# Block-local attention ahead of two expert layers: two query tiles at a time from tile 8 on

## The chip, the core and the metric

The kernel runs on one core of one Trainium2 chip. The metric is the device time of one execution in microseconds (us). TensorE (PE) multiplies matrices into PSUM, VectorE (DVE), ScalarE (ACT) and GpSimd (POOL) do the rest, and SyncE (SP) issues the transfers. Each engine runs its own instructions strictly in the order in which they were written, and waits at the head of its queue until another engine or a transfer has signalled.

## What is computed

Three stages follow one another. The attention is cut here to what matters; the other two only consume its output.

```python
# q, k, v: (2, 8, 768, 64); block 32, window 16
k_sum = k.reshape(B, H, nb, block, D).max(axis=3)
v_sum = v.reshape(B, H, nb, block, D).mean(axis=3)
scores_l = scale * q @ k^T, kept where abs(i - j) < window
scores_s = scale * q @ k_sum^T + log(block)
a = softmax(concat([scores_l, scores_s]))
attn = a @ concat([v, v_sum])
...
x  = attn as (1536, 512); x = sum over 8 experts of P[:, e] * (relu(x @ w1[e]) @ w2[e])
out = g(x @ w_in) @ w_out      # g a rational function
```

## The kernel before

**Tiles.** The 1536 rows of the attention are 24 query tiles of 64 rows, 12 in each batch entry (`QB = 12`). A tile `t` goes through five functions:

- `scores(t)`: 8 matmuls into a two-bank PSUM tile (`sc`), then 4 DVE reductions with the mask that write `a` and the row maxima `sm`.
- `exps(t)`: 4 ACT exponentials of `a`.
- `norm(t)`: three small DVE steps (add, reciprocal, multiply of `a`). Up to tile 16 their small results lie in spare columns of the bank of the last `xo` tile, later in `sm`.
- `trans(t)`: 4 PE transposes of `a` into a `tr` bank (`at`), and an ACT copy to `aT`. There are two `tr` banks, also used by half of the key and query transposes (`kps`, `qps`).
- `av(t)`: 8 matmuls of `aT` with the values `vx[t % 3]` into the only `xo` bank; an ACT cast to `xh` and a DVE difference to `xl`. `load_vx(t + 3)` then refills that value buffer by a transfer.

Each value is held as a rounded part and a remainder (`xh` and `xl`, `hh` and `hl`, `w2h` and `w2l`), and each product of the expert layers is three matmuls (lines 184 to 186).

**The main work.** The first expert's matmuls are cut into halves of 6 matmuls (`mains`): first-layer halves (`g1_halves`, 256 columns, written `p1`) and second-layer halves (`g2_halves`, 512 columns, `p2`). `share` says how many halves go with a step: 2, except 1 in steps 17, 18, 22 and 23. They fill PE between the attention's small matmuls. What empties a finished first-layer bank (ACT `hh`, DVE `hl`: a post) is put off: `flush()` writes it out at the next `av` or at the second half of the next product. The banks come from a pool of three (`psm`, `mm`), which the other half of the key and query transposes uses too.

**Order.** The program is written out by hand, step by step. Step `s` is: `scores(s)`, `av(s - 3)`, `flush()`, half the main work (before tile 12), `trans(s - 2)`, `norm(s - 1)`, `exps(s)`, then the step's list `todo[s]`, then the rest of the main work. `todo` holds the preparation of the second batch entry: key tiles are transposed and placed in steps 7 to 9 (`prep_k`), their edges copied and block maxima built in steps 8 to 10 (`halos`, `block_keys`, `blocks_to`), the means of its values in steps 9 to 13 (`sum_v`, `means_split`, `means_sum`, `block_values`), the second-layer weights split in steps 8 and 9 (`split_w2`), and query tiles placed in steps 10, 14 and 18 (`prep_q`).

Of the kernel before, what the change touches and what calls it, by code (L numbers as in the profile page):

```python
# [22 lines left out]
def kernel(  # L23
# [342 lines left out]
    with ExitStack() as actx:  # L366
# [229 lines left out]
        def load_vx(t):  # L596
# [5 lines left out]
                v[b, :, c0:c1, :].rearrange("h p d -> p h d"),  # L602
            )

        def scores(t):
            b, r = divmod(t, QB)
            qt = qT[b, r // TPL]
            if t == 1:
                ps = [psa.tile([P, NP, P], F32, tag="tr", name=f"sc_{t}_{x}", bufs=2) for x in range(2)]
            else:  # L610
                ps = psa.tile([P, 2, NP, P], F32, tag="sc", name=f"sc_{t}")
                ps = [ps[:, x] for x in range(2)]
            w = kw[:, slot(t)]
            i = 0 if r == 0 else (2 if r == QB - 1 else 1)
            m = masks[i]
            o = r % TPL * QT
            for p in range(NP):
                x = p % 2
                p = x * (NP // 2) + p // 2
                for j in range(2):  # L620
                    h = slice(j * D, (j + 1) * D)
                    y = (j ^ x) * D
                    nc.tensor.matmul(
                        ps[x][y:y + D, p % (NP // 2), 0:CO], lhsT=qt[h, p, o:o + QT], rhs=w[h, p, :],
                        start=True, stop=True, tile_position=(j * D, y),
                    )
            a = apool.tile([P, NP, CO], F32, tag="a", name=f"a_{t}", bufs=3)
            sm = apool.tile([P, 4, NP], F32, tag="sm", name=f"sm_{t}", bufs=3)
            for p in range(NP):
                p = p % 2 * (NP // 2) + p // 2  # L630
                nc.vector.tensor_tensor_reduce(
                    out=a[:, p, :], in0=ps[p // (NP // 2)][:, p % (NP // 2), 0:CO], in1=m[:, 0, :],
                    scale=-1.0, scalar=3.0e38, op0=ALU.add, op1=ALU.min, accum_out=sm[:, 0, p:p + 1],
                )
            st[t] = (a, sm, a)
# [32 lines left out]

        def av(t):
            aT = st.pop((t, "aT"))  # L670
            if t < 4 and t % 2:
                ps = psm.tile([P, NP * P], F32, tag="mm", name=f"xo_{t}").rearrange("p (c n) -> p c n", c=NP)
            else:
                ps = psa.tile([P, NP, P], F32, tag="xo", name=f"xo_{t}")
            for p in range(NP):
                for j in range(2):
# [4 lines left out]
                        rhs=aT[:, y:y + QT],  # L681
                        start=True, stop=True,
                    )
            st["xo"] = ps
            o = t * QT
            dh, dl = xh[:, :, o:o + QT], xl[:, :, o:o + QT]
            nc.scalar.copy(dh, ps[:, :, 0:QT])
# [142 lines left out]
            at(10 + i, means_split, i)  # L830
        at(13, means_sum)
        for t in range(QB, QB + 3):
            at(2 + t, block_values, t)
        at(13, gate_weights)
        at(13, gate_zeros)
        at(15, gate_parts)
# [7 lines left out]
        at(15, dma_sub, 0, 2)  # L844


        AV = 3
        mains = []
        for t0, n in ((0, 2 * P), (2 * P, 2 * P), (4 * P, 2 * P), (NT - HB, HB), (HT, HB)):
            ready = (t0 + n) // QT + AV  # L850
# [5 lines left out]
                    mains.append((ready, 0, f, NCH, h))  # L856
        share = dict(zip(range(7, 26), (2, 2, 2, 2, 2, 2, 2, 2, 2, 2, 1, 1, 2, 2, 2, 1, 1, 2, 2)))

        def main(s, end):
            n = share.get(s, 0)  # L860
            apart = n == 2 and s < QB
            for _ in range((1 if apart else n) if end else int(apart)):
                assert mains[0][0] <= s
                mains.pop(0)[2]()

        for s in range(NQ + AV):
            if s == 2:
                norm(0)
            if s < NQ:
                scores(s)  # L870
            if s == 2:
                prep_v(0, 0)
                prep_v(0, 1)
# [10 lines left out]
                prep_q(0, 1)  # L884
            if s >= AV:
                av(s - AV)
                if s - AV + 3 < NQ:
                    load_vx(s - AV + 3)
                flush()
            main(s, False)  # L890
            if AV < s < NQ + AV - 1:
                trans(s - AV + 1)
            if 2 < s < 6:
                spin(3)
            if AV < s <= NQ:
                norm(s - 1)
            if s < NQ and s not in (2, AV):
                exps(s)
            for f in todo.pop(s, []):
                f()  # L900
            main(s, True)
        assert not todo
        flush()
        assert not mains[0][4]
# [554 lines left out]
```

## Time and profile before

| | |
|---|---|
| time, median of 3 runs | 1352.11 us (1351.78 to 1352.18) |
| time of the profiled execution | 1352.21 us |
| its span, first to last instruction | 1350.5 us |
| busy share of the span: PE, DVE, ACT, POOL | 99%, 78%, 38%, 60% |
| share of the chain that ended last: PE, DVE, DMA | 97%, 1%, 1% |
| steps 8 to 23 of the attention | from 35.56 to about 95 us |

The profile lists, for one execution, what each engine did and when. Times of rows are us from the start of the span. The chain that ended last goes back from the last instruction to what released it, and so on: work off that chain can take longer at no cost. A matmul's record overlaps the next one's, so what a matmul costs is read from the distance of two starts, not from its duration; the same holds for neighbouring instructions of DVE and ACT.

### The profile page before, as it was taken

The page shows a single profiled execution, that of the slowest core. Times are in us where ns is not written, and L with a number is a line of the kernel's source. Part 1 is how long each engine was busy: PE and PEld are TensorE (multiplying, and loading weights), DVE is VectorE, ACT ScalarE, POOL GpSimd, SP SyncE. Part 2 cuts the span into 40 slices and gives each one's busy share as a digit, 9 for nine tenths or more (in the row PEclk, how much of TensorE's full clock was granted, in tenths as well). Part 3 has the DMA queues.
Part 4 walks back from the last instruction along what each step waited for, and adds up shares of the span by engine and source line. Part 5 has one row for each costly group of instructions (what it writes and reads, how often), then busy time and mean ns, then how long its engine had stood idle before and what let it go on. Part 6 is the DMA issues. An engine that isn't in the chain of part 4 may idle for free.

```text
span 1350.5 us, 20263 instructions
## 1 busy us (share of the span) xinstructions
PE 1342.1 (99%) x7343; PEld 1186.0 (88%) x7343; DVE 1052.9 (78%) x1956; ACT 510.9 (38%) x1136; POOL 804.3 (60%) x983
## 2 busy tenths in 40 slices
PE   8999999999999999999999999999999999999999
PEld 6888898999999999999999999999999888888887
DVE  7775588777777777777787777777777689988885
ACT  6874313222222222222222222222222379866662
POOL 7625747777776777776777767777777012222221
PEclk9999999999999999999999999999999999999999
DMA  9730112222222222222222222222222411312102
GB/s 262 169 85 1 51 46 63 89 70 79 67 73 68 67 77 67 83 66 87 69 77 72 67 74 68 76 69 77 75 80 62 146 57 47 94 33 94 32 16 78
DMA packets 122004, 102.40 MB, mean 76 GB/s; under 512 B 36272, under 2 KB 102960, under 8 KB 121904
## 3 DMA queue, kind: packets, MB, share of 16 engines
q1 hardware_dynamic: 121904, 101.10, 25.7%
q8 instruction: 58, 0.95, 0.3%
q14 instruction: 42, 0.34, 0.1%
HBM read 81.15 MB, written 19.92 MB: 75 GB/s over the span
## 4 chain that ended last, share of the span: by engine, by line
PE 97%; DVE 1%; DMA 1%; ACT 0%; SPq 0%; issue 0%; POOL 0%; DVEq 0%; ACTq 0%
PE p_v L185 12%; PE p_v L184 12%; PE p_v L186 12%; PE p L184 8%; PE p L186 8%; PE p L185 8%; PE X L1234 6%; PE X L1232 6%; PE X L1233 6%; PE Z L1233 3%; PE Z L1234 3%; PE Z L1232 3%; PE Y L1234 2%; PE Y L1233 2%; PE Y L1232 2%; PE xo L678 1%
## 5 line engine op out<-in xcount | busy, mean ns | idle before, releaser
L1347 DVE SCALAR_TENSOR_TENSOR accs<-p_v,Pt,accs 128x512 f32<-128x512 f32 x336 | 244.4, 746 | 85.9 <-PE p_v L186 85.2
L184 PE MATMUL p_v<-w2h_v,hh_v 128*128 128x512 f32 x720 | 282.2, 392 | 0.1
L186 PE MATMUL p_v<-w2h_v,hl_v 128*128 128x512 f32 x720 | 281.9, 392 | 0.0
L185 PE MATMUL p_v<-w2l_v,hh_v 128*128 128x512 f32 x720 | 281.7, 391 | 0.0
L1241 DVE SCALAR_TENSOR_TENSOR hl_v<-s,hh_v 128x384 fp32r<-128x384 f32 x180 | 137.4, 763 | 76.0 <-ACT hh_v L1240 74.6
L234 POOL TENSOR_TENSOR hl<-ta,hh 128x512 fp32r<-128x512 f32 x48 | 62.5, 1302 | 204.4 <-ACT hh L233 150.0
L1252 ACT COPY s<-X 128x384 f32<-128x384 f32 x56 | 27.0, 482 | 406.6 <-PE X L1234 406.6
L1041 POOL TENSOR_SCALAR ce<-ce 128x296 uint32<-128x296 uint32 (+1 forms) x56 | 67.1, 1199 | 176.7 <-DVE ce L1032 176.7
L186 PEld LDWEIGHTS p_v<-w2h_v,hl_v 128*128 128x128 f32 x720 | 135.2, 188 | 28.3
L184 PEld LDWEIGHTS p_v<-w2h_v,hh_v 128*128 128x128 f32 x720 | 135.4, 188 | 26.3 <-DVE accs L1342 0.5
L185 PEld LDWEIGHTS p_v<-w2l_v,hh_v 128*128 128x128 f32 x720 | 135.3, 188 | 25.9
L1240 ACT ACTIVATE hh_v<-s 128x384 fp32r<-128x384 f32 x180 | 94.9, 527 | 126.8 <-DVE s L1275 68.6
L110 POOL TENSOR_TENSOR wS<-S,wS 128x256 fp32r<-128x256 f32 x120 | 100.2, 835 | 14.4 <-ACT wS L107 4.7
L184 PE MATMUL p<-xh,w1h 128*128 128x512 f32 (+2 forms) x272 | 100.8, 371 | 0.0
L186 PE MATMUL p<-xh,w1l 128*128 128x512 f32 (+2 forms) x272 | 99.1, 364 | 0.0
L185 PE MATMUL p<-xl,w1h 128*128 128x512 f32 (+2 forms) x272 | 99.1, 364 | 0.0
L184 PE MATMUL p<-w2h,hh 128*128 128x512 f32 (+1 forms) x240 | 94.0, 392 | 0.0
L186 PE MATMUL p<-w2h,hl 128*128 128x512 f32 (+1 forms) x240 | 93.3, 389 | 0.0
L185 PE MATMUL p<-w2l,hh 128*128 128x512 f32 (+1 forms) x240 | 93.2, 388 | 0.0
L110 POOL TENSOR_TENSOR w2l_v<-sb,w2h_v 128x512 fp32r<-128x512 f32 x60 | 82.9, 1382 | 5.0
L1234 PE MATMUL X<-th,wS 128*128 128x384 f32 x240 | 80.3, 335 | 0.0
L1232 PE MATMUL X<-th,wS 128*128 128x384 f32 x240 | 80.3, 335 | 0.0
(249 smaller groups left out, 3309.1 us busy)
## 6 DMA issues: line engine op xcount, KB each, us to landing
sa<-in_moe_w_dram SPq DMA_DIRECT2D x30, 512.0 KB, 3.4
sb<-in_moe_w_dram SPq DMA_DIRECT2D x30, 512.0 KB, 4.3
cv<-in_moe_w_in_dram SPq DMA_DIRECT2D x24, 296.0 KB, 2.9
w1h<-f_in SPq DMA_DIRECT2D x16, 256.0 KB, 2.8
w1l<-f_in SPq DMA_DIRECT2D x16, 256.0 KB, 3.2
w2h<-f_out SPq DMA_DIRECT2D x16, 256.0 KB, 4.9
w2l<-f_out SPq DMA_DIRECT2D x16, 256.0 KB, 5.1
vx<-in_v_dram SPq DMA_DIRECT2D x20, 192.0 KB, 4.2
```

Source lines behind the costliest of these rows:

```text
L110: nc.gpsimd.tensor_sub(lo, src, hi.bitcast(F32))
L184: nc.tensor.matmul(ps, lhsT=sh, rhs=mh, start=(i == 0), stop=False)
L185: nc.tensor.matmul(ps, lhsT=sh, rhs=ml, start=False, stop=False)
L186: nc.tensor.matmul(ps, lhsT=sl, rhs=mh, start=False, stop=(i == n_k - 1))
L234: nc.gpsimd.tensor_sub(hl[:, :n], ta, hh[:, :n].bitcast(F32))
L1041: nc.gpsimd.tensor_scalar(out=e, in0=e, scalar1=896, scalar2=0, op0=ALU.subtract, op1=ALU.max)
L1232: nc.tensor.matmul(ps, lhsT=w[:, 0, t], rhs=mh, start=start and t == 0, stop=False, **go)
L1233: nc.tensor.matmul(ps, lhsT=w[:, 0, t], rhs=ml, start=False, stop=False, **go)
L1234: nc.tensor.matmul(ps, lhsT=w[:, 1, t], rhs=mh, start=False, stop=t == 1, **go)
L1240: nc.scalar.activation(hh, src, AF.Relu)
L1241: nc.vector.scalar_tensor_tensor(out=hl, in0=src, scalar=0.0, in1=hh.bitcast(F32), op0=ALU.max, op1=ALU.subtract)
L1347: nc.vector.scalar_tensor_tensor(out=a, in0=ps, scalar=Pt[:, g, e:e + 1], in1=a, op0=ALU.mult, op1=ALU.add)
```

## The change

From tile 8 on, steps are taken in pairs (`pair(s)` for even `s`). A pair is: `scores(s)`, `scores(s + 1)`, `exps(s)`, `av(s - 3)`, `av(s - 2)`, `norm(s)`, `flush()`, a quarter of the pair's main work, `exps(s + 1)`, `trans(s - 1)`, a quarter, `todo[s]`, a quarter, `trans(s)`, `todo[s + 1]`, a quarter, `norm(s + 1)`. The second tile's scores take the two `tr` banks in place of the two `sc` banks, and the odd tiles' `av` takes a bank of the pool of three. Before the first pair `trans(6)` and `norm(7)` are brought forward. The values of the block means (`block_values`) are copied a step earlier. No arithmetic is added or removed.

```diff
@@ -602,10 +602,13 @@
                 v[b, :, c0:c1, :].rearrange("h p d -> p h d"),
             )
 
+        AV = 3
+        PAIR = 8
+
         def scores(t):
             b, r = divmod(t, QB)
             qt = qT[b, r // TPL]
-            if t == 1:
+            if t == 1 or t > PAIR and t % 2:
                 ps = [psa.tile([P, NP, P], F32, tag="tr", name=f"sc_{t}_{x}", bufs=2) for x in range(2)]
             else:
                 ps = psa.tile([P, 2, NP, P], F32, tag="sc", name=f"sc_{t}")
@@ -668,7 +671,7 @@
 
         def av(t):
             aT = st.pop((t, "aT"))
-            if t < 4 and t % 2:
+            if t % 2 and (t < 4 or t >= PAIR - 3):
                 ps = psm.tile([P, NP * P], F32, tag="mm", name=f"xo_{t}").rearrange("p (c n) -> p c n", c=NP)
             else:
                 ps = psa.tile([P, NP, P], F32, tag="xo", name=f"xo_{t}")
@@ -681,7 +684,8 @@
                         rhs=aT[:, y:y + QT],
                         start=True, stop=True,
                     )
-            st["xo"] = ps
+            if t < PAIR - 3 or t % 2 == 0:
+                st["xo"] = ps
             o = t * QT
             dh, dl = xh[:, :, o:o + QT], xl[:, :, o:o + QT]
             nc.scalar.copy(dh, ps[:, :, 0:QT])
@@ -830,7 +834,7 @@
             at(10 + i, means_split, i)
         at(13, means_sum)
         for t in range(QB, QB + 3):
-            at(2 + t, block_values, t)
+            at(1 + t, block_values, t)
         at(13, gate_weights)
         at(13, gate_zeros)
         at(15, gate_parts)
@@ -844,7 +848,6 @@
         at(15, dma_sub, 0, 2)
 
 
-        AV = 3
         mains = []
         for t0, n in ((0, 2 * P), (2 * P, 2 * P), (4 * P, 2 * P), (NT - HB, HB), (HT, HB)):
             ready = (t0 + n) // QT + AV
@@ -856,18 +859,45 @@
                     mains.append((ready, 0, f, NCH, h))
         share = dict(zip(range(7, 26), (2, 2, 2, 2, 2, 2, 2, 2, 2, 2, 1, 1, 2, 2, 2, 1, 1, 2, 2)))
 
-        def main(s, end):
-            n = share.get(s, 0)
-            apart = n == 2 and s < QB
-            for _ in range((1 if apart else n) if end else int(apart)):
+        def main(s, n):
+            for _ in range(n):
                 assert mains[0][0] <= s
                 mains.pop(0)[2]()
 
-        for s in range(NQ + AV):
+        def pair(s):
+            n = [share[s], share[s + 1]]
+            two = s < NQ
+            if two:
+                scores(s)
+                scores(s + 1)
+                exps(s)
+            for t in (s, s + 1):
+                av(t - AV)
+                if t < NQ:
+                    load_vx(t)
+            if two:
+                norm(s)
+            flush()
+            main(s, n[0] // 2)
+            if two:
+                exps(s + 1)
+            trans(s - 1)
+            main(s, n[0] - n[0] // 2)
+            for f in todo.pop(s, []):
+                f()
+            main(s + 1, n[1] // 2)
+            if two:
+                trans(s)
+            for f in todo.pop(s + 1, []):
+                f()
+            main(s + 1, n[1] - n[1] // 2)
+            if two:
+                norm(s + 1)
+
+        for s in range(PAIR):
             if s == 2:
                 norm(0)
-            if s < NQ:
-                scores(s)
+            scores(s)
             if s == 2:
                 prep_v(0, 0)
                 prep_v(0, 1)
@@ -884,21 +914,27 @@
                 prep_q(0, 1)
             if s >= AV:
                 av(s - AV)
-                if s - AV + 3 < NQ:
-                    load_vx(s - AV + 3)
+                load_vx(s)
                 flush()
-            main(s, False)
-            if AV < s < NQ + AV - 1:
+            main(s, int(share.get(s) == 2))
+            if AV < s:
                 trans(s - AV + 1)
             if 2 < s < 6:
                 spin(3)
-            if AV < s <= NQ:
+            if AV < s:
                 norm(s - 1)
-            if s < NQ and s not in (2, AV):
+            if s not in (2, AV):
                 exps(s)
             for f in todo.pop(s, []):
                 f()
-            main(s, True)
+            main(s, int(share.get(s) == 2))
+        trans(PAIR - 2)
+        norm(PAIR - 1)
+        for s in range(PAIR, NQ + 2, 2):
+            pair(s)
+        av(NQ - 1)
+        for f in todo.pop(NQ + 2, []):
+            f()
         assert not todo
         flush()
         assert not mains[0][4]
```

Three places show how instructions move. The names end in the tile's number and a running number: `sc_9_1_703` is the second bank of tile 9's scores, `at_6` tile 6's transposes, `xo_5` its `av`, `p1_0_0_1` the first-layer product of the first rows with weight column 1, `a_8` tile 8's exponentials.

PE, where step 7 ends. Before:

```order
L186 MATMUL p1_0_0_0_0_626<-xh_90,w1l_0_0_480 128x256
L623 MATMUL sc_8_677<-kw_102,qs0_106 64x120 x8
L678 MATMUL xo_5_692<-aT_5_638,vx2_105 64x64 x8
L184 MATMUL p1_0_0_1_0_706<-xh_90,w1h_0_1_482 128x256
L185 MATMUL p1_0_0_1_0_706<-xl_91,w1h_0_1_482 128x256
L186 MATMUL p1_0_0_1_0_706<-xh_90,w1l_0_1_483 128x256
L184 MATMUL p1_0_0_1_0_706<-xh_90,w1h_0_1_482 128x256
L185 MATMUL p1_0_0_1_0_706<-xl_91,w1h_0_1_482 128x256
L186 MATMUL p1_0_0_1_0_706<-xh_90,w1l_0_1_483 128x256
L659 MATMUL at_6_713<-ident_84,a_6_547 120x128 x4
```

Now:

```order
L186 MATMUL p1_0_0_0_0_626<-xh_90,w1l_0_0_480 128x256
L662 MATMUL at_6_677<-ident_84,a_6_547 120x128 x4
L626 MATMUL sc_8_687<-kw_102,qs0_106 64x120 x8
L626 MATMUL sc_9_0_702<-kw_102,qs0_106 64x120 x2
L626 MATMUL sc_9_1_703<-kw_102,qs0_106 64x120 x2
L626 MATMUL sc_9_0_702<-kw_102,qs0_106 64x120 x2
L626 MATMUL sc_9_1_703<-kw_102,qs0_106 64x120 x2
L681 MATMUL xo_5_722<-aT_5_638,vx2_105 64x64 x8
L681 MATMUL xo_6_734<-aT_6_682,vx0_103 64x64 x8
```

Tile 6's transposes stand ahead of tile 8's scores, tile 9's scores follow at once in the two `tr` banks, and two `av` stand together.

ACT, from step 8 to the scores of tile 10 (`hh_0_0_1` is the post of `p1_0_0_1`, `w2h` the second-layer weights, `kw` the keys). Before:

```order
L687 CAST xh_90<-xo_6_777 128x4x64
L262 ACTIVATE hh_0_0_1_760<-p1_0_0_1_0_706 128x256
L661 COPY aT_7_803<-at_7_798 120x512
L641 ACTIVATE a_9_771,sm_9_772<-a_9_771,sm_9_772 128x120 x4
L440 ACTIVATE kw_102<-kps_1_2_0_818 128x16x32
L107 CAST w2h_0_2_830<-s2_0_1_651 128x512
L107 CAST w2h_0_3_834<-s2_0_1_651 128x512
L687 CAST xh_90<-xo_7_862 128x4x64
L262 ACTIVATE hh_0_0_2_845<-p1_0_0_2_0_791 128x256
```

Now, from tile 9's exponentials on:

```order
L644 ACTIVATE a_9_712,sm_9_713<-a_9_712,sm_9_713 128x120 x4
L664 COPY aT_7_767<-at_7_762 120x512
L440 ACTIVATE kw_102<-kps_1_1_0_784 128x16x32
L107 CAST w2h_0_0_796<-accs_92 128x512
L107 CAST w2h_0_1_800<-accs_92 128x512
L664 COPY aT_8_816<-at_8_811 120x512
L440 ACTIVATE kw_102<-kps_1_2_0_824 128x16x32
L107 CAST w2h_0_2_836<-s2_0_1_651 128x512
L107 CAST w2h_0_3_840<-s2_0_1_651 128x512
L262 ACTIVATE hh_0_0_1_775<-p1_0_0_1_0_751 128x256
L644 ACTIVATE a_10_867,sm_10_868<-a_10_867,sm_10_868 128x120 x4
L691 CAST xh_90<-xo_7_893 128x4x64
```

The post `hh_0_0_1` stood ahead of `aT_7` and of all that follows; now it stands behind two `aT`, two key copies and the four weight casts, and tile 10's exponentials behind it.

DVE, the same stretch (`hl_0_0_1` is the other half of that post, `ks` the block maxima, the three rows with `sm` and `a` a `norm`, ISA a reduction of scores). Before:

```order
L688 TENSOR_TENSOR xl_91<-xo_6_777,xh_90 128x4x64
L263 SCALAR_TENSOR_TENSOR hl_0_0_1_761<-p1_0_0_1_0_706,hh_0_0_1_760 128x256
L651 TENSOR_SCALAR xo_6_777<-sm_8_687 128x4
L652 RECIPROCAL xo_6_777<-xo_6_777 128x4
L653 TENSOR_TENSOR a_8_686<-a_8_686,xo_6_777 128x480
L480 TENSOR_REDUCE ks_1_655<-kw_102 128x4x8
L438 TENSOR_SCALAR kw_102<-kps_1_2_1_824 128x16x32
L631 ISA a_10_856,sm_10_857<-sc_10_847,mask1_111 128x120
```

Now:

```order
L480 TENSOR_REDUCE ks_1_655<-kw_102 128x4x8
L438 TENSOR_SCALAR kw_102<-kps_1_2_1_830 128x16x32
L263 SCALAR_TENSOR_TENSOR hl_0_0_1_776<-p1_0_0_1_0_751,hh_0_0_1_775 128x256
L654 TENSOR_SCALAR xo_6_734<-sm_9_713 128x4
L655 RECIPROCAL xo_6_734<-xo_6_734 128x4
L656 TENSOR_TENSOR a_9_712<-a_9_712,xo_6_734 128x480
L634 ISA a_10_867,sm_10_868<-sc_10_858,mask1_111 128x120
```

`hl_0_0_1` stood ahead of the block maxima and the key copy and now stands behind them; the `norm` of tile 9 and the reductions of tile 10 wait behind it.

## Rows read from the trace of the kernel before

**Rows 1.** Windows: steps 8 to the last `av`; us, then busy us of each engine.

```profile
35.56:102.79 67.23, 67.05 (x872) 56.48 (x871) 49.61 (x218) 53.63 (x201) 28.67 (x38) 1.00 0.52 120
102.79:1350.50 1247.71, 1244.40 (x6131) 1105.91 (x6127) 976.64 (x1625) 432.31 (x848) 749.94 (x881) 1.00 0.22 68
```

**Rows 2.** Timeline of PE, end of step 7: start, duration, line, tiles, count.

```profile
35.23 0.28 PE L185 MATMUL p<-xl,w1h 128*128 128x256 f32 x1
35.35 0.28 PE L186 MATMUL p<-xh,w1l 128*128 128x256 f32 x1
35.56 0.64 PE L623 MATMUL sc<-kw,qs 64*64 64x120 f32 x16
```

**Rows 3.** Timeline of PE, step 15, and a second-layer half of step 11.

```profile
65.71 0.64 PE L623 MATMUL sc<-kw,qs 64*64 64x120 f32 x16
66.28 0.69 PE L678 MATMUL xo<-aT,vx 120*64 120x64 f32 x16
66.90 0.65 PE L659 MATMUL at<-ident,a 128*120 128x128 f32 x4
67.31 0.36 PE L184 MATMUL p<-xh,w1h 128*128 128x256 f32 x1
67.51 0.28 PE L185 MATMUL p<-xl,w1h 128*128 128x256 f32 x1
...
49.11 0.50 PE L184 MATMUL p<-w2h,hh 128*128 128x512 f32 x1
...
50.60 0.60 PE L659 MATMUL at<-ident,a 128*120 128x128 f32 x4
```

**Rows 4.** Timeline of ACT, step 7: the two key copies and what follows them.

```profile
36.15 1.15 ACT L440 ACTIVATE kw<-kps 128x512 f32<-128x512 f32 x2
37.19 0.36 ACT L687 CAST xh<-xo 128x256 fp32r<-128x256 f32 x1
```

**Rows 5.** Timeline of ACT: step 15 whole, and two weight casts of step 8.

```profile
40.81 1.11 ACT L107 CAST w2h<-accs 128x512 fp32r<-128x512 f32 x2
...
67.01 0.37 ACT L687 CAST xh<-xo 128x256 fp32r<-128x256 f32 x1 [0.81 <-PE xo L678]
67.28 0.39 ACT L262 ACTIVATE hh<-p 128x256 fp32r<-128x256 f32 x1
67.64 0.59 ACT L661 COPY aT<-at 120x512 f32<-120x512 f32 x1
68.12 0.40 ACT L641 ACTIVATE a<-a,sm 128x120 f32<-128x120 f32 x1
...
69.65 0.19 ACT L356 ACTIVATE coef<-coef 128x2 f32<-128x2 f32 x1
```

**Rows 6.** Timeline of DVE: step 15, and the block maxima of step 9.

```profile
43.88 1.21 DVE L480 TENSOR_REDUCE ks<-kw 128x32 f32<-128x1024 f32 x1
...
66.42 0.28 DVE L631 CUSTOM_DVE_ANT_0 a<-sc,mask 128x120 f32<-128x120 f32 x1 [0.73 <-PE sc L623]
...
67.23 0.08 DVE L631 DVE_READ_ACCUMULATOR2_ANT sm<- 128x1 f32 x1
67.42 0.42 DVE L688 TENSOR_TENSOR xl<-xo,xh 128x256 fp32r<-128x256 f32 x1
...
68.09 0.15 DVE L651 TENSOR_SCALAR xo<-sm 128x4 f32<-128x4 f32 x1
...
68.50 0.66 DVE L653 TENSOR_TENSOR a<-a,xo 128x480 f32<-128x480 f32 x1
```

**Rows 7.** Timeline of POOL, steps 11 and 12: block maxima copied, value sums.

```profile
50.37 0.53 POOL L388 TENSOR_SCALAR kw<-ks 128x384 f32<-128x384 f32 x1
50.84 1.31 POOL L547 TENSOR_TENSOR accs<-v 128x512 f32<-128x512 f32 x1
```

**Rows 8.** Timelines: a `norm` of DVE in step 18, and POOL at that time.

```profile
75.09 4.27 POOL L785 TENSOR_TENSOR accs<-accs 128x384 f32<-128x384 f32 x4
...
77.30 0.99 DVE L651 TENSOR_SCALAR sm<-sm 128x4 f32<-128x4 f32 x1
...
78.53 1.34 DVE L653 TENSOR_TENSOR a<-a,sm 128x480 f32<-128x480 f32 x1
```

**Rows 9.** The tile `vx`, steps 4 to 23: its transfers.

```profile
DMA to landing us min/median/max: 2.3/2.9/6.5
```

## The prediction

> **What bounds the kernel now.** First the windows. From step 8 to the last `av`, 67.23 us, PE is busy 67.05 us, and after that 1244.40 of 1247.71 [rows 1]. The reader is to see two things: PE waits for almost nothing in the stretch that the change touches, so there is little to win; and nothing behind it can take up a delay, so a wait added here arrives whole at the end. In the same stretch ACT is busy 53.63 and DVE 49.61 of 67.23: they have slack on average, but not at every moment. Next the timelines, for what a step costs PE. The scores take 0.57, `av` 0.62, the transposes 0.41 (distances of starts, 65.71 to 67.31) [rows 3]. The first main matmul behind them takes 0.20, a later one 0.12, and the last one ahead of scores 0.21 [rows 2, 3]: entering the main work costs 0.08, leaving it 0.09. A first-layer half is so 0.80, a second-layer half 1.49 (49.11 to 50.60) [rows 3].
>
> The other engines' steps. ACT [rows 5]: cast 0.27, post 0.36, copy to `aT` 0.48 (ready after 0.59), four exponentials 1.53 (68.12 to 69.65), weight cast about 0.53; a key copy 0.52 [rows 4]. DVE [rows 6]: reductions 0.14 behind the scores, 0.89 for four (each done alone after about 0.3), `xl` and post together 0.67, `norm` 1.07 (68.09 to 69.16), block maxima 1.21.
>
> **The change, part by part.** Arithmetic is the same; what moves is the order, so I follow the new order with these durations, on the clock of the trace before.
>
> *Switches.* Counted in the order from tile 8 on, main work is entered 29 times instead of 23, and left for scores or `av` 9 times instead of 19: 6 x 0.08 less 10 x 0.09 is 0.4 us gained. The 0.18 us in which PE idled [rows 1] may go too. That is the whole gain in sight, 0.6.
>
> *Pair 8.* Step 7's last main matmul starts at 35.35 [rows 2]. Tile 6's transposes now run from 35.5 to 35.9, tile 8's scores to 36.5. Tile 9's scores need both `tr` banks. One holds tile 6's transposes, whose copy to `aT` stands on ACT behind two key copies that end at 37.19 [rows 4]; it is ready at 37.8. PE waits 1.2 us, and the scores end at 38.3. Before, that copy hid behind a step of main work. PE then needs two `av` 1.24, four halves 3.2, two transposes 0.82, 16 key transposes (four times 0.41) 1.64, one exit 0.09: the pair ends at 45.3.
>
> *Pair 10.* ACT has from 37.2: three `aT` 1.44 (tiles 6, 7, 8), two sets of exponentials 3.06, two casts 0.54, a post 0.36, two key copies 1.04, four weight casts 2.12, together 8.6, and reaches the post `hh_0_0_1` at 45.8. DVE stands at `hl_0_0_1` until 46.2, and behind it are `norm(9)`, done at 47.7, and tile 10's reductions. `av(8)` needs the only `xo` bank, which holds `norm(9)`'s small results: PE is there at 47.1 and waits 0.6. Tile 10's exponentials start at 47.9, though ACT is free from 46.2; they end at 49.5, the casts at 50.0, two `xl` at 50.6, `norm(10)` at 51.7, and `hl_0_0_2` frees a bank of the three at 52.0. PE wants one for `p2_0_0` at 51.2 (47.7 + 0.62 + 0.80 + 0.41 + 0.80 + 0.82): a wait of 0.8. The block maxima end at 53.2, POOL copies them (0.53) and only then sums the values `sum_v(1, 1)` (1.31) [rows 7], 55.1; ACT's cast of that sum stands ahead of the post `hh_0_0_3`, 56.0, which the second half of `p2_0_0` reads. PE is there at 54.7 (52.0 + 1.49 + 0.41 + 0.75): 1.3. Pair 10 loses 2.7 in all.
>
> *Plain pairs.* `norm(s + 1)` is the last thing of a pair on DVE, behind the post `hl`, whose ACT half stands behind `aT(s)`. Counted from the start of tile `s`'s transposes: `aT` 1.0, post 1.4 and 1.75, `norm` 2.8. The next scores are done at 1.9, so their reductions start 0.8 late, exponentials run from 3.1 to 4.65, casts to 5.2, two `xl` to 5.7, `norm(s + 2)` to 6.75. PE reaches tile `s + 2`'s transposes at 6.45 with four first-layer halves on the way: a wait of 0.3. Where a half is missing ahead of them it is longer: 1.5 in pair 16; in pair 22, with two halves in all, 0.7 at tile 21 and 1.3 at tile 22. Where other PE work lies between there is less: 0.1 in pair 12, 0.3 in pair 14, none in pair 20 behind a second-layer half. In pair 18 the second half of `p2_0_2` reads `hl_256_3`, a post flushed in the same pair behind `norm(18)`: PE is there 4.1 after the pair's start (1.14 + 1.24 + 0.41 + 1.3), the post, by the same chain of scores, exponentials, casts, `xl` and `norm`, is done at 5.4: 1.3.
>
> Sum of waits: 1.2 + 2.7 + 0.1 + 0.3 + 1.5 + 1.3 + 0 + 2.0 = 9.1; less 0.6: **+8.5 us**. Bounds, since the trace of before shows none of these waits: at least those that the order makes in any case, 1.2 in pair 8, 1.3 in pair 10 and 1.0 in pair 18, 3.5 less 0.6 is +2.9. At most each of eight pairs 0.3 longer and one `norm` stretched by POOL: 9.1 + 2.4 + 1.5 - 0.6 = +12.4. I take the worked value.
>
> That stretch: beside POOL's additions, which read SBUF, a `norm` on `sm` took 2.57 (77.30 to 79.87) instead of 1.07 [rows 8]. Before, it cost nothing. In the new order it hits `norm(17)`, and I find it done at 82.5, before it is wanted; if POOL is a little later it also hits `norm(18)`, ahead of `hl_256_3`, and PE pays the 1.5.
>
> The Trainium skill, page "SBUF — State Buffer", section "Who interferes with whom", says that a VectorE instruction with two SBUF inputs and a GpSimd instruction that reads SBUF exclude each other, so that the second fully blocks until the first is done. By that rule a `norm` could wait for one whole POOL addition at its multiply, and the sum would be up to about 1 us more for each `norm` that meets POOL. The multiply's 1.34 against 0.66 agrees with it.
>
> *At nothing.* `block_values` a step earlier is POOL work in a stage where POOL is busy 28.67 of 67.23 [rows 1]; the first still follows the value means, by my sums about 1 us ahead of the `av` that reads it. The transfer of an even tile's values is issued behind its `av` and used one pair later, 6.5 us or more (1.14 + 1.24 + 3.2 + 0.82 + 0.09), where it had three steps. Landing took 2.9, at most 6.5 [rows 9]; without that cover it is the last rival below.
>
> **Rivals.** *Only the key pairs lose.* ACT and DVE run the plain pairs a few tenths faster than I add up, and pairs 12 to 22 hold little. For it: each of those waits is a margin of 0.3 to 1.5 in a chain of five waits. Against it: two of them follow from the order of posts alone. Pairs 8 and 10 give 3.9, plain pairs up to 1.5, less 0.6: 1355.5 to 1357.0 us.
>
> *Not slower: the banks are free in time.* Tile 9's scores have banks of their own, so PE needn't wait for the emptying of others. This decides at ACT: if the copy to `aT` of tile 6 were ready at 36.6 and not 37.8, and the post `hh_0_0_1` before 45.2, DVE would not be held and the first four waits of the list would go; what stays is about 1.3 in pair 10, and two equal blocks in a row may save another 0.1 to 0.2 a pair. That gives 1351 to 1354 us; faster than 1349.4 it is only if PE waits nowhere. Against it: the two key copies that end at 37.19 [rows 4] stand ahead of that copy as before.
>
> The Trainium skill, page "Perfetto Trace Analysis", section "Matmuls", advises that independent groups of matmuls rotate through different PSUM banks, so that one is emptied while the next is computed; by it the second score tile would cost nothing. The rows on ACT speak against it here, since the banks are not empty when they are wanted.
>
> *More: values late.* An even tile's transfer queues on SP behind a load that waits for its buffer, and lands after the `av` that wants it. At 6.5 us to landing [rows 9] against 6.5 to 7.5 available it costs 1 to 2 us in several pairs: 1365 to 1370 us.
>
> **How the numbers follow.** The profiled execution took 1352.21 us, 0.1 above the median shown, so the prediction is 1352.2 + 8.5 = 1360.7 us. Chances: the forecast (1357 to 1365) 0.64, only the key pairs 0.18, not slower 0.11, values late 0.07. The range from 1355 to 1365 takes in the forecast and the first rival, 0.82. Within 0.2% is 1349.4 to 1354.8, about what a measurement of this kernel can tell from no change: of the third case three quarters lie there, the rest below. Slower 0.89, same 0.08, faster 0.03.
>
> **What would show it.** In the profile after, PE's waits in the attention should appear, where there were none: tile 9's scores for ACT by 1.2, `av(8)` and `p2_0_0` for DVE, `p2_0_0`'s second half for ACT, `at(16)`, `at(21)` and `at(22)` for DVE, `p2_0_2` for DVE. ACT should show `hh_0_0_1` near 45.8 and DVE an idle time of about 1 us ahead of `hl_0_0_1`. The last `av` should end 8 to 9 us later, and the stretch behind it should be as long as before. Wrong would be a stretch with PE as busy as before [rows 1], or a loss that arises behind the attention.

## The result, and the profile after

The changed kernel takes 1359.60 us (median of six, 1359.43 to 1360.07) against 1351.95 for the kernel before: 7.65 us more, a ratio of 1.0057 with the 95% interval 1.0046 to 1.0067. Forecast were 1360.7, in a range from 1355 to 1365.

First the windows of the profile after, cut where those of before were [rows 1]: from the end of step 7 to the first main matmul behind the last `av`, and from there to the end. Columns as there: length, then busy us of PE, its weight loads, DVE, ACT, POOL, then the granted clock, the share of DMA and GB/s.

```profile
35.55:110.36 74.81, 66.16 (x871) 56.03 (x870) 49.02 (x218) 53.22 (x201) 28.82 (x38) 1.00 0.46 108
110.36:1358.00 1247.64, 1244.45 (x6131) 1105.26 (x6127) 975.89 (x1625) 432.96 (x848) 750.57 (x881) 1.00 0.22 68
```

The attention has grown from 67.23 to 74.81, by 7.58; the rest is as long as before (1247.64 against 1247.71). PE is busy 0.89 less than before (66.16 against 67.05) and idle 8.65 where it was idle 0.18. DVE, ACT and POOL have the same work in a longer stretch, so no engine has become the bound on average.

The view of PE's waits, which had none in this stretch before, now lists eleven. The timeline of PE shows them in order (start, duration, line, tiles, count, idle time before and what ended it):

```profile
36.10 1.05 PE L626 MATMUL sc<-kw,qs 64*64 64x120 f32 x20
37.70 0.63 PE L626 MATMUL sc<-kw,qs 64*64 64x120 f32 x12 [0.55 <-ACT aT L664]
38.26 1.15 PE L681 MATMUL xo<-aT,vx 120*64 120x64 f32 x32
...
45.02 1.05 PE L626 MATMUL sc<-kw,qs 64*64 64x120 f32 x32
46.00 0.69 PE L681 MATMUL xo<-aT,vx 120*64 120x64 f32 x16
47.52 0.69 PE L681 MATMUL xo<-aT,vx 120*64 120x64 f32 x16 [0.83 <-DVE a L656]
...
51.88 0.50 PE L184 MATMUL p<-w2h,hh 128*128 128x512 f32 x1 [0.63 <-DVE hl L263]
...
54.29 0.40 PE L186 MATMUL p<-w2h,hl 128*128 128x512 f32 x1
55.78 0.50 PE L184 MATMUL p<-w2h,hh 128*128 128x512 f32 x1 [1.10 <-ACT hh L262]
56.12 0.40 PE L185 MATMUL p<-w2l,hh 128*128 128x512 f32 x1
...
70.88 0.39 PE L184 MATMUL p<-xh,w1h 128*128 128x256 f32 x1 [0.41 <-DVE hl L263]
...
75.11 0.69 PE L681 MATMUL xo<-aT,vx 120*64 120x64 f32 x16 [0.50 <-issue]
...
79.17 0.62 PE L662 MATMUL at<-ident,a 128*120 128x128 f32 x4 [1.26 <-DVE a L656]
...
83.47 0.62 PE L662 MATMUL at<-ident,a 128*120 128x128 f32 x4 [0.23 <-DVE sm L634]
...
86.18 0.50 PE L186 MATMUL p<-w2h,hl 128*128 128x512 f32 x1 [0.83 <-DVE hl L263]
...
100.13 0.62 PE L662 MATMUL at<-ident,a 128*120 128x128 f32 x4 [1.19 <-DVE sm L634]
...
102.59 0.62 PE L662 MATMUL at<-ident,a 128*120 128x128 f32 x4 [1.12 <-DVE a L656]
```

The reader is to see that a wait hides in a busy row, too. Two scores in a row take 0.98 (45.02 to 46.00), but in pair 8 they last from 36.10 to 38.26: 1.18 is lost there, of which the view shows 0.55. Another 0.44 is in the 1.05 of the first row, whose 20 matmuls would take 0.61 at the pace of the 32, and 0.19 is in the second, whose 12 take 0.56 (37.70 to 38.26) and not 0.37. By pairs, with the idle time of the view for all but pair 8: 1.18 (pair 8), 0.83 + 0.63 + 1.10 (pair 10), 0.41 (pair 14), 0.50 + 1.26 (pair 16), 0.23 + 0.83 (pair 18), 1.19 + 1.12 (pair 22); nothing in pairs 12 and 20.

Why the engines that it waits for are late is seen best in pair 22. First ACT, then DVE:

```profile
95.79 1.05 ACT L664 COPY aT<-at 120x512 f32<-120x512 f32 x2
96.74 0.39 ACT L262 ACTIVATE hh<-p 128x256 fp32r<-128x256 f32 x1
```

```profile
97.16 0.42 DVE L263 SCALAR_TENSOR_TENSOR hl<-p,hh 128x256 fp32r<-128x256 f32 x1 [1.76 <-ACT hh L262]
97.50 0.16 DVE L654 TENSOR_SCALAR sm<-sm 128x4 f32<-128x4 f32 x1
...
98.48 0.28 DVE L634 CUSTOM_DVE_ANT_0 a<-sc,mask 128x120 f32<-128x120 f32 x1
```

ACT makes the post `hh` only behind two copies to `aT`. DVE stands idle 1.76 for it, with `norm(21)` and then the reductions of tiles 22 and 23 behind it in its queue. The reductions empty the `tr` bank in which `at_21` is to be written, and so PE waits 1.19 at `at_21` (100.13). `at_22`, which wants the `norm(22)` that follows from those reductions, waits 1.12.

### The profile page after: what moved, and what is told of

The parts are those of the page before. It is cut to its first block, busy times and chain, and to the rows that moved or that the text cites. A ratio compares the mean times of both kernels' runs of the same rounds, so it can differ in the third digit from the quotient of the medians.

```text
span 1358.1 us, 20261 instructions
## 1 busy us (share of the span) xinstructions
PE 1341.1 (99%) x7343; PEld 1184.5 (87%) x7343; DVE 1051.6 (77%) x1956; ACT 511.4 (38%) x1136; POOL 805.1 (59%) x983
## 4 chain that ended last, share of the span: by engine, by line
PE 93%; DVE 3%; ACT 2%; DMA 1%; POOL 1%; issue 1%; SPq 0%; ACTq 0%; DVEq 0%; POOLq 0%
PE p_v L185 12%; PE p_v L186 12%; PE p_v L184 12%; PE p L184 8%; PE p L186 8%; PE p L185 8%; PE X L1270 6%; PE X L1268 6%; PE X L1269 6%; PE Z L1270 3%; PE Z L1269 3%; PE Z L1268 3%; PE Y L1270 2%; PE Y L1269 2%; PE Y L1268 2%; ACT a L644 1%
## 5 line engine op out<-in xcount | busy, mean ns | idle before, releaser
L1270 PE MATMUL X<-th,wS 128*128 128x384 f32 x240 | 80.2, 334 | 0.0
L1269 PE MATMUL X<-tl,wS 128*128 128x384 f32 x240 | 80.2, 334 | 0.0
```

The source lines that it names most:

```text
L1269: nc.tensor.matmul(ps, lhsT=w[:, 0, t], rhs=ml, start=False, stop=False, **go)
L1270: nc.tensor.matmul(ps, lhsT=w[:, 1, t], rhs=mh, start=False, stop=t == 1, **go)
```

## The experiments

Each time below is a median beside that of the kernel before on the same chip (1351.80 to 1351.95); the changed kernel is 7.65 above. "Above" is the difference to it.

| kernel | us | above | ratio (95%) |
|---|---|---|---|
| pairs from tile 12 | 1358.24 | 6.3 | 1.0041 (1.0028 to 1.0055) |
| norm(s + 1) early | 1357.63 | 5.7 | 1.0043 (1.0030 to 1.0055) |
| value split a step later | 1361.16 | 9.3 | 1.0065 (1.0052 to 1.0077) |
| order of before, banks of after | 1357.95 | 6.0 | 1.0043 (1.0031 to 1.0056) |
| four moves | 1354.82 | 3.0 | 1.0024 (1.0015 to 1.0033) |
| posts early | 1356.15 | 4.4 | 1.0034 (1.0022 to 1.0047) |
| order of before, `tr` banks | 1357.09 | 5.3 | 1.0039 (1.0026 to 1.0051) |
| order of before, `mm` banks | 1353.21 | 1.4 | 1.0011 (1.0002 to 1.0020) |
| three moves | 1354.28 | 2.5 | 1.0019 (1.0009 to 1.0028) |
| three moves, half ahead | 1353.65 | 1.9 | 1.0014 (1.0005 to 1.0022) |
| that order without the key copy, from tile 12 | 1352.86 | 1.1 | 1.0008 (0.9999 to 1.0016) |
| that order without the key copy, from tile 20 | 1351.87 | 0.0 | 1.0001 (0.9991 to 1.0010) |

My theory was that the loss is made of waits for posts and norms that stand in the wrong order in the queues of ACT and DVE. The rivals: that only the key pairs lose; that DVE is short of time in any order; that the shared banks cost by themselves.

**Where the loss lies.** Pairs from tile 12 on.

```diff
-        PAIR = 8
+        PAIR = 12
```

> The pairing begins at tile 12 and not at tile 8; tiles 8 to 11 run one at a time as in the kernel before. Theory (each lost microsecond is a wait in a named pair, and the two key pairs hold 1.1 for the second score tile and 0.83 + 0.63 + 1.10 in pair 10): 3.7 go, and the cheaper score and av blocks of two pairs, about 0.6, go too, so 1356.5 us, 4 to 5 above before. Rival 'only the key pairs lose': 1351 to 1353 us. Rival 'pairing costs in itself, in each pair the same': a quarter of the loss goes, 1357.7 us, and the waits of pairs 8 and 10 would turn up in pair 12.

Of the five runs, two took 1356.80 and 1357.02, 0.3 to 0.5 above the theory's 1356.5; the other three took 1358.24 to 1358.34, by a drop of TensorE's clock that the last section shows. "Only the key pairs lose" is refuted either way: without them 4.9 and more of the 7.65 are left. The waits of pairs 14 to 22 are there with the same sizes (0.40, 0.50, 1.25, 0.23, 0.82), and the one of the second score tile came along to tile 13 (0.58), which the theory had not foreseen. The last rival, the same cost in each pair, doesn't hold: the three waits of pair 10 turn up nowhere.

**The odd tile's norm, early.**

```diff
             if two:
                 exps(s + 1)
+                norm(s + 1)
             trans(s - 1)
...
             main(s + 1, n[1] - n[1] // 2)
-            if two:
-                norm(s + 1)
```

> norm(s + 1) is written right behind exps(s + 1) and so stands on VectorE ahead of the posts of its pair, not behind them. Theory (the plain pairs lose because the next reductions and the odd tile's norm queue behind a post that waits for ScalarE): the waits at at(16) 1.26, at(21) 1.19, at(22) 1.12, av(8) 0.83 and the ones of 0.2 to 0.4 go in the main, the post of pair 18 in part; 1355 to 1356.5 us. Rival (VectorE is simply short of time there, whichever order): the posts come later instead and the second-layer halves wait, so 1358.5 us or more. Rival (POOL's additions stretch the norm): the waits of pairs 16 and 18 stay.

1357.63, that is 1.9 of the loss taken back and not 3 to 4.5. The waits of `av(8)`, `av(14)` and pair 14 are gone and that of `at(21)` is down to 0.23. But those of `at(22)` (1.13) and of the second-layer half in pair 18 (0.83) stay, a wait of 0.66 at the key transposes in pair 8 is new (the view puts it down to POOL's `w2l`), and of the next two the first has doubled and the second is little shorter. PE in pairs 10 and 16:

```profile
55.53 0.50 PE L184 MATMUL p<-w2h,hh 128*128 128x512 f32 x1 [2.08 <-ACT hh L262]
...
77.68 0.62 PE L662 MATMUL at<-ident,a 128*120 128x128 f32 x4 [1.05 <-DVE a L656]
```

In pair 10 the post `hh_0_0_3` comes when GpSimd's value sum lets it (55.10 here, 55.35 in the changed kernel), so PE, which arrives earlier, waits longer. `at(16)` waits for `norm(16)` of its own pair, which this move doesn't touch; that norm's first step and multiply took 0.17 and 0.65, so POOL didn't stretch it.

**The cast ahead of that post.**

```diff
-            at(10 + i, means_split, i)
+            at((10, 12, 12)[i], means_split, i)
```

> The split of the value sum of key tile 1 (ScalarE's cast and GpSimd's subtraction) moves from step 11 to step 12, so that ScalarE's post hh_0_0_3 no longer stands behind a cast that waits for GpSimd. Theory: the 1.10 that TensorE waits for that post in pair 10 goes and nothing takes its place: 1358.5 us. Rival (ScalarE's post would be late anyway, by VectorE's freeing of the bank): 1359.2 to 1359.6 us, with a wait for hl in its place.

The theory fell here. The median is 1361.16, with the drop of the clock in three of five runs; the two without it took 1359.8, so nothing is gained. PE in pairs 10 and 12:

```profile
54.63 0.50 PE L184 MATMUL p<-w2h,hh 128*128 128x512 f32 x1 [0.32 <-ACT hh L262]
...
63.12 0.65 PE L587 MATMUL vps<-vhl,wavgr 128*24 128x512 f32 x2 [0.21 <-POOL vhl L578]
64.38 0.41 PE L587 MATMUL vps<-vhl,wavgr 128*24 128x512 f32 x1 [0.61 <-POOL vhl L578]
```

The 1.10 has become 0.32, but the value means now wait 0.21 + 0.61 for GpSimd's half of the split: a delay paid in another place.

**The posts, early.** A post is issued ahead of the other work of its step, so that it passes that cast and the copies without moving them away.

```diff
             main(s, n[0] - n[0] // 2)
+            flush()
             for f in todo.pop(s, []):
...
                 trans(s)
+            flush()
             for f in todo.pop(s + 1, []):
```

> Posts alone are flushed ahead of the other work of both steps of a pair. Theory: the 1.10 at hh_0_0_3 goes, since the post no longer stands behind the cast that waits for GpSimd's sum, and 0.2 to 0.4 of the wait of pair 14: 1358 to 1358.6 us. Rival (the half that reads it waits for VectorE then, hl_0_0_3, or the cast's delay comes out at the value means two pairs later): 1359.2 to 1359.8 us.

1356.15: 3.3 taken back, at least twice what I expected. The 1.10 of pair 10 is gone with only 0.28 at the value means, and so is the 0.83 of pair 18; `at(16)` waits 0.78 and not 1.26, `at(21)` 0.70 and not 1.19; only the transposes in pair 18 wait longer, 0.77 and not 0.23. In the attention DVE idles 5.1 at the head of its queue for a late `hh`, where it idled 8.1, and what stands behind it is earlier. Of the moves tried alone on the changed kernel, this one took back most.

**All together.** Four moves: `norm(s + 1)` early, posts early, `norm(s)` ahead of the pair's `av` with its small results in `sm`, and the second copy of key tile 0 on DVE, which frees ACT for `aT` of tile 6.

```diff
-                place(kT[b, i], par, transpose8("k", b, i, par), 1.0, i == 0)
+                place(kT[b, i], par, transpose8("k", b, i, par), 1.0)
...
                 exps(s)
+                norm(s)
...
-            if two:
-                norm(s)
             flush()
...
-            if t < NS + 1:
+            if t < PAIR:
                 o = st["xo"]
```

> Four moves against the changed kernel's waits at once: both norms of a pair are written right behind their exponentials (norm(s) ahead of the pair's av, its small results in sm instead of the xo bank, norm(s + 1) ahead of the posts); posts are flushed ahead of the other work of both steps, so that ScalarE reaches hh_0_0_3 before the cast of the value sum; and the second copy of the first key tile is VectorE's and not ScalarE's. Theory (the loss is these waits and nothing else): the 8.7 of waits fall to 1 or less, while the cheaper blocks stay: 1350 to 1352.5 us, at or under the kernel before. Rival (taking the scores' banks from the transposes costs in any order, as in the run with the banks alone): not under 1355. Rival (the xl behind norm(s) are then late for the main work): waits of the first-layer halves for xl, 1354 to 1357.

1354.82, above what I expected: the waits that the view lists in the pairs fell to 4.5, not to 1. The first rival's 1355 is just undercut, and the second came true in one place, a wait of 1.61 at the query transposes in pair 10, whose bank an odd `av` holds until DVE has made its `xl`. DVE, and then POOL, show why that was late:

```profile
47.99 0.96 DVE L654 TENSOR_SCALAR sm<-sm 128x4 f32<-128x4 f32 x1 [0.28 <-ACT a L644]
...
49.20 1.47 DVE L656 TENSOR_TENSOR a<-a,sm 128x480 f32<-128x480 f32 x1
```

```profile
46.40 2.53 POOL L110 TENSOR_TENSOR w2l<-s,w2h 128x512 fp32r<-128x512 f32 x2
48.87 1.28 POOL L547 TENSOR_TENSOR accs<-v 128x512 f32<-128x512 f32 x1
```

The first step of `norm(10)` ends when POOL's subtractions do (48.95 and 48.93), and its multiply ends about 0.5 after POOL's sum (50.67 and 50.15). So the same move without `norm(s)`:

> The run with four moves less one of them: norm(s) stands behind the pair's xl again and uses the xo bank, as in the changed kernel; kept are norm(s + 1) behind its exponentials, the posts ahead of the other work, and the key copy on VectorE. Theory (each move is worth the waits that it takes, and norm(s) ahead of the xl only traded its gain for the 1.61 at the query transposes, whose bank an odd av holds until its xl): 1353 to 1354.3 us. Rival (norm(s) early was the move that paid): 1355.5 us or more.

1354.28, at the upper end of what was expected; the rival is refuted. The 1.61 is gone, and the norm's first step and its multiply take 0.17 and 0.65 again beside the same work of POOL. The view no longer lists a wait of tile 9's scores, but the first row shows that the two scores of pair 8 last 1.46 (35.95 to 37.41) and not 0.98: of the 1.18 about 0.5 is left. That row, and PE's waits in the pairs of this kernel:

```profile
35.95 1.53 PE L626 MATMUL sc<-kw,qs 64*64 64x120 f32 x32
...
47.83 0.62 PE L662 MATMUL at<-ident,a 128*120 128x128 f32 x4 [0.50 <-DVE sm L634]
50.67 0.50 PE L184 MATMUL p<-w2h,hh 128*128 128x512 f32 x1 [0.63 <-DVE hl L263]
...
62.51 0.42 PE L587 MATMUL vps<-vhl,wavgr 128*24 128x512 f32 x1 [0.58 <-POOL vhl L578]
...
75.79 0.62 PE L662 MATMUL at<-ident,a 128*120 128x128 f32 x4 [0.78 <-ACT a L644]
80.10 0.62 PE L662 MATMUL at<-ident,a 128*120 128x128 f32 x4 [0.23 <-DVE sm L634]
94.62 0.62 PE L662 MATMUL at<-ident,a 128*120 128x128 f32 x4 [0.23 <-DVE sm L634]
97.08 0.62 PE L662 MATMUL at<-ident,a 128*120 128x128 f32 x4 [1.12 <-DVE a L656]
```

So three moves in the queues of ACT and DVE take back 5.2 of 7.65, with every bank as in the changed kernel. The key copy was not tried by itself; what changed in pair 8 is its likely share.

**A half ahead of the transposes.** To that:

```diff
-            main(s + 1, n[1] // 2)
+            main(s + 1, (n[1] + 1) // 2)
...
-            main(s + 1, n[1] - n[1] // 2)
+            main(s + 1, n[1] // 2)
```

> As the run without norm(s) moved, and where a pair's second step has one half of main work alone (pairs 16 and 22), it stands ahead of trans(s) and not behind it. Theory (the waits at at(16) and at(22) are the time that a missing half leaves uncovered): about 0.8 less at each, 1.3 to 1.6 in all, so 1352 to 1353 us. Rival (the wait moves to the next transposes or scores, since VectorE's chain is as long as before): no gain, or under 0.4.

1353.65, a gain of 0.6 between theory and rival. The wait of `at(16)` is gone and that of `at(22)` 0.41; but now `trans(s)` stands directly ahead of the next scores, which want the banks that it has just filled. The transposes in pair 18 wait 0.66 and not 0.23, and the scores there last 1.30 to the next start and not 0.98:

```profile
76.86 1.37 PE L626 MATMUL sc<-kw,qs 64*64 64x120 f32 x32
```

**The banks alone.** The order of before, one tile at a time, with odd scores in the `tr` banks and odd `av` in the `mm` banks; then each alone.

```diff
-            if t == 1:
+            if t == 1 or t > 8 and t % 2:
                 ps = [psa.tile([P, NP, P], F32, tag="tr", name=f"sc_{t}_{x}", bufs=2) for x in range(2)]
...
-            if t < 4 and t % 2:
+            if t % 2 and (t < 4 or t >= 5):
                 ps = psm.tile([P, NP * P], F32, tag="mm", name=f"xo_{t}").rearrange("p (c n) -> p c n", c=NP)
...
-            st["xo"] = ps
+            if t < 5 or t % 2 == 0:
+                st["xo"] = ps
...
-            at(2 + t, block_values, t)
+            at(1 + t, block_values, t)
```

> The kernel before with the banks of the changed kernel alone: odd tiles' scores from 9 on in the two tr banks, odd av from tile 5 on in the mm banks, the block values a step earlier; the order stays one tile at a time. Theory (the order costs, not the banks): within 0.7 us of before, 1351.5 to 1352.7. Rival (the shared banks cost by themselves): at least half of the loss, 1355.5 us or more.

> One part of the run with the banks alone: the kernel before, with the scores of odd tiles from 9 on in the two tr banks and nothing else. If the tr banks carry that run's loss (its waits at the second half of tile 9's and 11's scores for key and query copies, 0.8 and 0.7, and the transposes that wait for reductions): 1355.5 us or more. If the av banks do: within 1 us of before.

> The other part: the kernel before, with odd av from tile 5 on in the mm banks and the block values a step earlier. If the tr banks carry the loss of the run with both: within 0.7 us of before, 1351.3 to 1352.6. If the mm banks do (three of them, which the posts free): 1354.5 us or more.

The theory fell in this form, and the rival came true: the banks alone cost 6.0, the `tr` banks 5.3 and the `mm` banks 1.4, which lies between the two cases of the last expectation. With the `tr` banks alone PE waits for copies of the keys and queries that share them, and its busy time grows by stalls inside the score rows to 68.99 (67.05 before):

```profile
40.52 0.63 PE L623 MATMUL sc<-kw,qs 64*64 64x120 f32 x12 [0.82 <-ACT kw L440]
...
50.00 0.63 PE L623 MATMUL sc<-kw,qs 64*64 64x120 f32 x12 [0.83 <-ACT qs L440]
```

```profile
35.16:107.68 72.52, 68.99 (x872) 57.24 (x871) 49.72 (x218) 54.08 (x201) 28.65 (x38) 1.00 0.49 114
```

It doesn't follow that 5.3 of the changed kernel's loss is due to these banks: the two orders want them at other times, and with the banks unchanged the queues gave back 5.2. What it shows is that they aren't free: a transpose and a score tile each wait until the other's results are read.

**A later start of the better order.** `norm(s + 1)` early, posts early and the half ahead, from tile 12 and from tile 20. In the second, steps up to 19 keep their halves as before:

```diff
-            main(s, int(share.get(s) == 2))
+            n = share.get(s, 0)
+            ahead = int(n == 2 and s < QB)
+            main(s, ahead)
...
-            main(s, int(share.get(s) == 2))
+            main(s, n - ahead)
```

> The paired order of the run before it (norm(s + 1) and posts early, the single half ahead of trans(s)), but from tile 12 on, with both key copies on ScalarE as in the kernel before. Theory (key and query copies, weight casts and block maxima crowd the two key pairs; a plain pair with its waits removed saves 0.2 to 0.3 by its blocks in a row): at or below the kernel before, 1350.8 to 1352.2 us. Rival (the paired order costs in every pair, through the tr banks that scores now share): 1353 us or more.

> The paired order of the run from tile 12 on (norm(s + 1) and posts early, the single half ahead of trans(s)), but from tile 20 on; tiles up to 19 run one at a time, with their halves as in the kernel before. In that run the stretch from tile 20's scores to the end of the attention was 0.7 shorter than in the kernel before (18.27 against 18.97), while all that stands ahead of tile 20 had lost 1.8. Theory (a pair gains where the halves around it cover its chains): 0.3 to 0.7 under the kernel before, 1351.1 to 1351.6 us. Rival (the entry into the pairs, where tile 21's scores wait for the aT of tile 18, costs what the two pairs gain): 1351.7 to 1352.4 us.

From tile 12: 1352.86, between theory and rival, 0.1 short of the rival's 1353. PE's waits that are left:

```profile
PE at L662 <- DVE sm L634: 0.9, 2, 0.6
PE sc L626 <- ACT aT L664: 0.6, 1, 0.6
PE at L662 <- DVE a L656: 0.4, 1, 0.4
PE vps L587 <- POOL vhl L578: 0.3, 1, 0.3
```

1.5 of these 2.2 are waits for a bank: transposes for the reductions, scores for `aT`. More is hidden in busy rows: the scores of pair 12 last 0.97 longer than elsewhere, of which 0.56 is listed, and those of pair 18 0.32 longer. From tile 20: 1351.87 against 1351.83, no change; tile 20's and 21's scores lasted 1.35 there, not 0.98, and two waits of 0.23 and 0.41 were left. So the theory fell in both. In the second the rival's time came: the two pairs give no more than their entry and those waits cost. No version beat the kernel before, and what the order could gain with the `tr` banks left to the transposes was not tried.

## Why the prediction was right

**What bounds it, and that a delay arrives whole:** right. 7.58 of the 7.65 are in the attention (8 to 9 were forecast for the end of the last `av`), and the stretch behind it is as long as before.

**The waits:** their places and causes were right in the main, and the sum is close, 9.1 forecast and 9.28 by the list above. By pairs, forecast and measured: pair 8 1.2 and 1.18; pair 10 2.7 and 2.56; pair 12 0.1 and 0; pair 14 0.3 and 0.41; pair 16 1.5 and 1.76; pair 18 1.3 and 1.06; pair 20 nothing in either; pair 22 2.0 and 2.31. The chain in pair 10 came as worked out: ACT reached `hh_0_0_1` at 45.62 (forecast 45.8), `norm(9)` was done at 47.46 (47.7), and ACT began `hh_0_0_3` at 55.35, so that PE went on at 55.78 (56.0). DVE stood idle 0.67 ahead of `hl_0_0_1` (about 1). That this order of posts and norms is the cause was an argument then; the early posts and norms and the key copy have shown it for 5.2 of the 7.65. That the sum comes so close is in part luck: in pairs 16 and 18 unforeseen waits of 0.50 and 0.23 make up for forecast ones that came 0.24 and 0.47 too short. The lower bound, +2.9, counts 1.0 for pair 18 where the sum has 1.3, without a reason; with 1.3 it is +3.2.

**Where it was off in place:** `at(21)` doesn't wait for `norm(21)`, as I had it, but for the `tr` bank that tile 23's scores still hold; the norm is only what stands ahead of the reductions that empty it. Pair 14's wait was forecast at the transposes and came at a first-layer half that wants a bank, and pair 16 has a wait that I had not: `av(14)` for the `xo` bank, until `norm(15)` is done with its small results (74.35 + 0.65; PE's 75.11 is about that end, though the view names no releaser; with the odd norm early this wait is gone).

**Switches:** the term that was mis-sized. I took 0.6 for what the order saves; 9.28 - 7.58 leaves 1.7. Two scores in a row take 0.98, where two single ones take 1.14 by [rows 3], and two `av` take 1.08 (57.66 to 58.74) against 1.24. That is 0.32 in a pair, which I had put at 0.1 to 0.2 and only in a rival. Eight pairs of scores and the seven of nine `av` pairs that no wait cut give 2.4; with the 0.6 that is 3.0, more than 1.7.

The trace shows where the difference goes: a wait costs more than the idle time that the view gives it. Ahead of the 1.10 in pair 10 the matmul at 54.29 counts as busy for 0.40, where in a stream the next one starts after 0.23; behind it the first takes 0.34 (55.78 to 56.12) and not 0.23. That is 0.27 more. Counted so, against the same neighbours where no wait lies between them, the ten waits of pairs 10 to 22 cost 0.04 to 0.27 more each, 1.8 in all (an estimate from the distances of starts). By the distances that the forecast adds up, the waits are then 11.1 and not 9.1, and the order saves 3.5 and not 0.6: 1.3 in the scores, 1.3 in the `av`, 0.75 in the transposes (18 take 6.82, before 7.57) and the 0.18 of old idle time. The two errors, 2.0 and 2.9, cancel in part; that the total came within 0.85 of the forecast is luck to that extent.

**At nothing:** `block_values` and the values' transfers cost nothing; no wait in the list is for them. The transfers of `vx` in steps 4 to 23 took a median of 3.3 us to landing (2.4 to 6.0), where it was 2.9 (2.3 to 6.5) [rows 9], and no `av` in the stretch waited for one.

**The rivals.** Values late: refuted, since PE never waits for a transfer there. Only the key pairs: refuted by 5.5 of waits in pairs 14 to 22 and by the first run from tile 12. Not slower, since the banks are free: refuted, and in the runs with the banks alone they cost 6.0 in the old order. The Trainium skill, page "Perfetto Trace Analysis", section "Matmuls", wants independent groups of matmuls in different PSUM banks in turn. Here the second score tile had other banks, but they were taken from the transposes, and in the old order that alone cost 5.3.

**The norm beside POOL:** `norm(17)` was hit, as forecast, and done before it was wanted (81.17; forecast 82.5); `norm(18)` escaped. DVE in pairs 16 and 18:

```profile
79.28 0.32 DVE L654 TENSOR_SCALAR sm<-sm 128x4 f32<-128x4 f32 x1
...
79.84 1.33 DVE L656 TENSOR_TENSOR a<-a,sm 128x480 f32<-128x480 f32 x1
...
84.73 0.16 DVE L654 TENSOR_SCALAR sm<-sm 128x4 f32<-128x4 f32 x1
...
85.14 0.66 DVE L656 TENSOR_TENSOR a<-a,sm 128x480 f32<-128x480 f32 x1
```

The first is 0.83 longer than the second (0.16 and 0.67), and PE paid nothing for it.

## What to carry to other kernels

When two tiles are issued together, list for each in-order engine what stands ahead of the instruction that PE will want next: here 3.3 of the 7.65 us came back by two lines that issued small posts earlier. Read what a wait costs from the starts around it, since part of it can stand in a busy row. Count the banks that the second tile takes from others as a cost of its own, to be tried alone with the old order. Taking a delay away gains nothing where PE then only waits longer at a point that another engine fixes, as at the value sum here.

## What the runs showed of the hardware

**The granted clock can fall behind two short waits.** In the first run from tile 12 on (1358.24), PE in pair 22 (timeline; the three windows below it have the clock behind POOL's column):

```profile
97.11 0.62 PE L662 MATMUL at<-ident,a 128*120 128x128 f32 x4 [1.19 <-DVE sm L634]
...
99.57 0.82 PE L662 MATMUL at<-ident,a 128*120 128x128 f32 x4 [1.13 <-DVE a L656]
...
101.60 1.90 PE L681 MATMUL xo<-aT,vx 120*64 120x64 f32 x32
103.43 0.39 PE L184 MATMUL p<-xh,w1h 128*128 128x256 f32 x1
```

```profile
95.00:99.50 4.50, 2.26 (x42) 1.94 (x38) 3.90 (x23) 3.72 (x18) 0.00 (x0) 1.00 0.36 82
100.00:103.00 3.00, 3.00 (x34) 2.78 (x34) 0.80 (x2) 1.00 (x3) 0.00 (x0) 0.50 0.00 0
103.50:108.00 4.50, 4.50 (x28) 3.98 (x28) 1.28 (x4) 1.63 (x4) 0.00 (x0) 1.00 0.01 4
```

PE was busy 2.26 of 4.50, then the clock was granted at 0.50, the lower of its two levels (1.2 GHz), for some 3 us, and at 1.00 again. The steps from `at(22)` to the main work took 3.86, where in the profile of the changed kernel, with the same two waits and a clock of 1.00, they took 2.35 (102.59 to 104.94): 1.5 more. That is about the difference between the runs of this kernel, 1356.8 and 1358.2. The changed kernel itself showed no such drop behind the same waits (busy 2.28 of 4.50, 98.00 to 102.50); why is open. The profile with the value split later shows the drop at the same place, behind waits of 1.19 and 1.13 (granted 0.51 from 103 to 106). That kernel and three others have runs with a mean clock of 0.998 or 0.999, too, 1.1 to 1.8 longer than their others: three of five (value split later), one of five each (odd norm early, posts early) and two of ten (four moves).

**A norm in SBUF ends with, or shortly behind, an instruction of POOL.** With the small results in `sm` its first step took 0.96 and its multiply 1.47, with them in the `xo` bank 0.17 and 0.65 beside the same POOL work. In the kernel before [rows 8], the changed kernel (`norm(17)`), the one with the odd norm early and the one with four moves, a first step in `sm` beside POOL ended 0.03 behind the end of a POOL instruction and the multiply behind it 0.51 after the end of the next. The Trainium skill, page "SBUF — State Buffer", section "Who interferes with whom", says that VectorE with two SBUF inputs and a GpSimd instruction that reads SBUF block each other for an instruction's length, and that `tensor_scalar` can enter a mode that takes both ports and so contends with GpSimd, under conditions on its operands. The rows agree with both: the multiply has two inputs in SBUF only with `sm`, and the first step, a `tensor_scalar`, was long only where it wrote to SBUF.
